# Four integer sums on GpSimd, another order of the first steps, and eight zero products on TensorE in a retention block with a SwiGLU network behind it

## The chip, the cores and the metric

The kernel runs on one core of a Trainium2 chip. A core has five engines that run their own instruction streams and wait for each other on semaphores: TensorE (PE in the profile, with its weight loads as PEld), VectorE (DVE), ScalarE (ACT), GpSimd (POOL) and SyncE (SP), which here only issues DMA transfers. The metric is the device time of one execution in microseconds (us).

## The reference

Two blocks follow each other. The first is a retention recurrence over 4 batches, 8 heads, 768 positions and 64 dimensions:

```python
gamma = 1.0 - 2.0 ** (-5.0 - np.arange(H, dtype=np.float32))
for t in range(S):
    state = gamma[None, :, None, None] * state + np.einsum('bhd,bhe->bhde', k[:, :, t], v[:, :, t])
    y[:, :, t] = scale * np.einsum('bhd,bhde->bhe', q[:, :, t], state)
```

Its output, as x of 3072 rows by 512, goes through a gated network with 1536 hidden columns:

```python
g = x @ w_gate
silu = g * (1.0 / (1.0 + np.exp(-g)))
val = x @ w_val
return (silu * val @ w_out)
```

The weights arrive as 64 bit floats (float64), everything else as 32 bit.

## The kernel before, in words

**Retention in chunks.** The 768 positions of a batch are cut into 6 chunks of 128. In a chunk the recurrence becomes products: scores k times q (step `s`, line L628, then a mask on VectorE, L634), the scores times v (`m`, L713), the old state times the decayed q (`o`, L699), and the update of the state from the decayed k and v (`t`, L684). k is scaled by `k` (GpSimd, L649) or `K` (VectorE), q by `q` or `Q` (L643), the old state by `g` (ACT, L670). Each product is a group of eight instructions in the program, sixteen in the trace. The work is done in 4 segments of 6 chunks (two batches at a time, three chunks of each).

**Numbers in three planes.** To keep 32 bit accuracy, an operand of the large products is split into three rounded planes: for weights `near_a` (ACT, L960), `near_b` (VectorE, L963) and `near_c` (GpSimd, L966), as the steps `n`; for x `far_a` (ACT, L969, inside `m`), `far_b` and `far_c` (VectorE, L399 and L976, the steps `x`). TensorE multiplies plane by plane, so a group of 12 products (3 planes by 4 blocks of 128) needs the third plane for its last four products.

**The first segment** computes gate and value products directly: for the first two hidden blocks of 128 columns in parts, chunk by chunk (`p` for the gate and `v` for the value, L906, twelve products with 256 columns each), then for the other ten in full (`G` and `W`, L888, 384 columns). Later segments use a scheme with seven instead of eight products (L1057), and the down products are L1126.

**Weights from their words.** A 64 bit weight is loaded as two 32 bit words and turned into a 32 bit float on the chip. For a piece, `U` and `V` load words with SP (L511), and the steps `a`, `b`, `S`, `c`, `C` convert them: `a` (ACT, L532) brings the upper word into range, `b` (ACT, L535) puts the sign into PSUM, `S` (VectorE, L545) shifts the bits and joins the sign, `c` (ACT, L538) makes an integer of the upper bits of the lower word, and `C` adds the two as integers. For pieces of the up weights `C` is on VectorE (L553, a custom operation on 16 bit halves), for those of the down weights on GpSimd (L555). The pieces of the first two hidden blocks are converted in two halves of 512 columns each, w_val and w_gate apart (a0:0, a0:1, ...), all others whole.

**What sets the order.** The engines' orders are written out: a text `PLAN` holds 2371 steps, and each step issues its instructions in that place on the engine that it uses. Names with a slash belong to later segments. `l0:2` is the load of operand 2 (0 k transposed, 1 q transposed, 2 v, 3 k by rows) of chunk 0; the first two loads of q are on ACT's queue, all others on SP's. `A0` to `A2` load the tables of masks and decays, `Z` writes converted weights back to DRAM, `T` forms sums of weights (L399), `u` and `y` are the gate's activation and product, `h0` copies a mask for later (L738), `L` loads two small tables. A DMA transfer has one of eight semaphores, used in turn; a transfer waits at its issue for the one eight places earlier to have landed. Ahead of the plan stand a warm-up of eight products of zeros (L1222) and the loading of an activation table.

Of the kernel before, what the change touches and what calls it, by code (L numbers as in the profile page):

```python
# [14 lines left out]
AF = mybir.ActivationFunctionType  # L15
# [10 lines left out]
L = 3  # L26
# [24 lines left out]
    l0:0 l1:0 A0 A1 s0 U0:0 l0:2 l0:3 a0:1 s1 b0:1 A2 h0 S0:1 m0 K0 x0:2 c0:1 l2:0 x0:1 l2:1 l1:3  # L51
    C0:1 t0 l1:2 V0:0 l3:1 n0:0 s2 a0:0 Q2 l3:0 l2:3 n0:1 b0:0 S0:0 m1 k1 x1:1 x1:2 l2:2 c0:0 n0:2
    U1:1 C0:0 t1 o2 l3:3 g2 s3 n0:3 n0:4 l4:1 p0:0 m2 a1:1 x2:1 k2 q3 b1:1 l4:0 a1:0 x2:2 S1:1 l5:1
    l3:2 n0:5 c1:1 k3 t2 C1:1 o3 b1:0 l5:0 l4:2 g3 v0:0 s4 S1:0 t3 l5:2 c1:0 C1:0 U2:0 m3 s5 U12:3
    U3:1 q5 q4 u0:0 a2 o5 o4 T0:0 n1:0 m4 b2 y0:0 x3:1 x3:2 m5 T0:1 n1:1 n1:3 T0:2 S2 n1:2 p0:1 v0:1
    n1:4 T1:0 x4:1 u0:1 y0:1 a12 n1:5 x5:1 U4:0 T1:1 a3 p1:0 x4:2 u1:0 p1:1 x5:2 Z0 u1:1 T1:2 c12
    v1:0 U5:1 y1:0 v1:1 p0:2 Z1 l5:3 v0:2 c2 C2 b12 y1:1 p1:2 n2:0 a4 U6:0 u0:2 b3 n2:1 u1:2 v1:2
    S12 n2:3 L y0:2 S3 c3 n2:2 U13:2 G2:0 n2:4 T2:0 G2:1 C3 y1:2 T2:1 n3:0 b4 n2:5 n3:1 i2:0 i2:1
    T2:2 W2:0 j2:0 n3:2 W2:1 G3:1 n3:3 S4 C12 a5 Z2 j2:1 Z12 n3:4 c4 C4 U7:1 n3:5 T3:0 T3:1 c13 T3:2
    G3:0 n4:0 n4:1 b5 S5 n4:2 W3:0 n4:3 W3:1 i3:0 i3:1 n4:4 a13 a6 G4:1 c5 Z3 b13 G4:0 T4:0 U8:0 C5  # L60
    T4:1 j3:1 n4:5 b6 U14:3 W4:1 n5:0 T4:2 n5:1 i4:1 n5:2 n5:3 j3:0 S6 i4:0 a7 c6 n5:4 W4:0 T5:0 C6
    G5:1 Z4 T5:1 n6:0 U9:1 j4:0 n5:5 S13 G5:0 a8 b7 n6:3 T5:2 j4:1 n6:1 c14 C13 W5:1 S7 i5:1 Z5 n6:4
    i5:0 n6:2 j5:1 c7 W5:0 G6:1 n6:5 l4:3 a9 U10:0 C7 n7:0 G6:0 j5:0 i6:1 T6:0 k4 b8 g4 Z13 n7:1
    n7:3 U15:2 S8 n7:2 W6:1 i6:0 c8 n7:4 T7:0 a14 W6:0 C8 T7:1 T6:1 b14 G7:1 U11:1 n8:0 n8:1 n7:5
    i7:1 T6:2 G7:0 j6:0 b9 S14 W7:0 h2 c15 j6:1 Z6 S9 C14 n8:3 c9 n8:2 i7:0 n8:4 W7:1 G8:1 T7:2 C9
    G8:0 j7:0 n8:5 a10 b10 n9:0 j7:1 n9:3 Z14 a15 W8:0 P2 W8:1 Z7 n9:4 k5 b15 i8:0 S10 T8:0 n9:1
    i8:1 U16:3 n9:5 c10 S15 P0 T8:1 n9:2 C10 a11 C15 G9:0 t4 G9:1 P1 T9:0 i9:0 T8:2 Z15 j8:1 g5 j8:0
    t5 W9:1 W9:0 b11 n10:0 U17:2 T9:1 c16 Z8 n10:3 1/was0.0 a16 i9:1 n10:1 n10:4 n10:2 b16 G10:1 S11
    n10:5 c11 S16 i10:1 G10:0 0/h0.0 j9:0 C16 Z16 C11 n11:0 W10:0 n11:3 a17 j9:1 i10:0 0/h0.1 b17
    T9:2 n11:4 T11:0 Z9 n11:1 T11:1 W10:1 n11:2 G11:1 T11:2 0/W0 n11:5 c17 Z11 0/h1.0 G11:0 j10:0  # L70
    0/d0.0 h1 0/h0.2 1/sc0 j10:1 i11:0 0/h1.1 0/W1 S17 0/d1.0 i11:1 0/d0.1 1/l3 C17 T10:0 1/dec0.0
    W11:0 0/d1.1 0/d0.2 W11:1 0/h2.0 j11:0 0/D0.2 j11:1 1/k0.0 1/l4 1/dec0.1 1/q0.0 0/D0.1 1/q0.1
    0/D0.4 1/k0.1 1/l5 0/D0.0 0/h2.1 0/d1.2 0/h1.2 0/h4.0 0/W2 0/Z0 1/A0 1/y0.06 1/new0.0 0/h4.1
    1/y0.01 0/D0.5 0/D0.3 0/d2.0 1/B0 0/D1.1 0/h3.0 1/y0.03 0/D1.5 1/y0.04 0/Z1 1/y0.02 1/y0.07
    1/y0.05 T10:1 1/was0.1 1/y0.15 1/y0.00 1/y0.14 0/d2.1 0/D1.4 1/y0.12 0/d2.2 0/D1.2 1/y0.13 0/W3
    Z17 0/D1.3 0/Z2 0/d3.0 0/D1.0 0/h2.2 0/h3.1 1/C0 0/W4 T10:2 0/h3.2 0/d3.1 0/h4.2 Z10 1/y0.16
    1/l7 1/y0.17 1/new0.1 1/sum0.0 0/D2.3 0/D2.1 1/y0.10 0/h5.0 1/begin 1/sum0.1 0/d3.2 0/h5.1
    1/y0.11 0/D2.5 1/sc1 0/D2.0 0/d4.0 1/was1.0 0/D2.4 0/d4.1 0/D3.4 1/l6 1/dec1.1 0/h5.2 1/dec1.0
    0/D2.2 1/x0.2.0 0/D3.1 1/q1.1 0/d4.2 0/W5 0/D3.5 1/x0.1.0 0/h6.0 1/k1.0 0/Z3 1/sum0.3 1/k1.1
    1/sum0.2 1/x0.2.1 0/D4.5 0/D3.2 0/D3.3 0/D3.0 1/q1.0 0/Z4 0/h6.1 0/D4.0 0/D4.4 1/x0.1.2 1/x0.1.1  # L80
    1/A1 1/x0.0.0 0/d5.0 1/x0.2.2 1/y1.00 0/h6.2 1/y1.06 1/x0.0.2 1/new1.0 0/D4.2 0/d5.1 0/d5.2
    0/D4.3 0/D4.1 1/y1.07 1/y1.01 0/W6 0/h7.0 1/B1 1/x0.0.1 1/y1.04 1/y1.12 0/h7.1 1/l9 0/d6.0
    0/D5.4 0/h8.0 0/d6.1 1/y1.02 0/D5.3 0/D5.2 0/W7 0/h8.1 1/y1.05 0/d6.2 1/l8 1/l11 0/Z5 1/y1.03
    1/was1.1 0/D5.5 1/C1 0/d7.0 1/y1.16 0/d7.1 0/D6.5 0/D5.0 1/y1.17 1/y1.15 1/new1.1 0/h7.2 1/y1.14
    1/y1.11 0/D5.1 1/y1.13 1/x1.2.0 0/D6.3 0/d7.2 0/D6.4 0/Z6 1/y1.10 0/D7.3 0/h9.0 1/sc2 0/h8.2
    1/x1.2.2 0/D6.2 1/q2.1 1/k2.1 0/D7.5 0/W8 1/sum1.0 0/D6.1 1/sum1.2 1/k2.0 0/D6.0 0/D7.1 1/x1.1.0
    0/h10.0 0/h9.1 0/d8.0 0/D7.2 1/dec2.0 1/l10 1/sum1.1 1/dec2.1 0/W9 1/x1.1.1 0/D7.0 0/d8.1
    1/x1.2.1 0/Z7 1/sum1.3 1/was2.0 1/q2.0 1/x1.0.0 1/x1.1.2 0/d9.0 0/D7.4 0/d8.2 0/h11.0 1/A2
    1/new2.0 0/D8.0 1/x1.0.1 0/h10.1 0/D8.3 0/D8.2 0/d9.1 1/L0 0/D8.1 1/y2.00 0/D8.4 1/B2 0/W10
    0/d9.2 1/y2.07 1/y2.05 0/d10.0 0/D8.5 0/h9.2 1/y2.02 0/h11.1 0/D9.3 1/y2.03 0/h10.2 1/y2.01  # L90
    0/D9.5 0/Z8 1/y2.04 1/y2.06 1/w0.0.0 0/D9.4 0/d10.1 0/h11.2 1/C2 1/y2.16 1/y2.14 0/W11 1/y2.12
    0/D9.1 1/y2.10 0/D9.2 1/L1 0/d10.2 0/D10.3 0/Z9 0/d11.0 1/y2.17 1/x1.0.2 1/y2.15 1/y2.13 0/D9.0
    1/L2 0/D10.4 0/D10.1 1/sum2.2 0/D10.2 0/D10.0 1/y2.11 0/d11.1 1/sum2.0 0/d11.2 1/x2.1.0 1/sum2.1
    1/x2.1.2 1/sum2.3 0/D11.1 0/Z11 1/w0.1.0 0/D11.0 1/x2.0.0 0/D11.3 0/D10.5 0/D11.4 1/w0.0.1
    0/D11.2 1/w0.0.2 1/w1.0.0 1/x2.1.1 1/x2.0.1 0/Z10 1/w1.0.1 0/e0 1/x2.0.2 1/w1.0.2 0/D11.5 1/p0.0
    1/u0.0 1/p0.1 1/p0.2 1/p1.0 1/x2.2.0 1/u0.1 1/w0.2.0 0/e2 1/x2.2.1 1/w0.1.1 1/p1.1 1/x2.2.2 0/e1
    1/w0.1.2 0/e3 1/w1.2.0 1/w1.1.0 1/w0.2.1 1/u1.0 1/w2.1.0 1/u0.3 1/p1.2 1/w1.1.1 1/p0.3 1/u0.4
    1/p0.4 1/w0.2.2 1/u0.5 1/p0.5 1/u0.6 1/w1.2.1 1/w2.0.0 1/w1.1.2 1/u1.3 1/p0.6 1/u0.8 1/p1.3
    1/w2.0.1 1/p1.4 1/u1.4 1/w2.0.2 1/u1.1 1/L3 1/u0.9 1/p1.5 1/p2.0 1/w2.2.0 1/w1.2.2 1/u1.5
    1/w3.2.0 1/u0.2 1/w2.1.1 1/w3.2.1 1/u1.2 1/w3.1.0 1/u1.6 1/u2.0 1/w3.0.0 1/w3.0.1 1/p1.6  # L100
    1/w2.1.2 1/p2.1 1/p2.3 1/w3.1.1 1/L4 1/p2.2 1/u1.8 1/u2.4 1/u2.1 1/u2.3 1/p2.5 1/w3.0.2 1/w4.2.0
    1/u1.9 1/u2.6 1/w2.2.1 1/p2.4 1/w3.2.2 1/L5 1/p3.1 1/w2.2.2 1/u2.5 1/u1.7 1/w4.1.0 1/w4.0.0
    1/u0.7 1/p3.0 1/u3.0 1/w3.1.2 1/w4.0.1 1/w4.1.1 1/p2.6 1/p3.2 1/u3.3 1/p3.3 1/p3.4 1/u3.4 1/u2.2
    1/u2.8 1/p3.5 1/u3.1 1/u3.5 1/L6 1/w5.1.0 1/p3.6 1/w4.0.2 1/u2.9 1/w4.1.2 1/u3.6 1/w5.0.0
    1/w4.2.1 1/p4.1 1/w5.0.1 1/p4.0 0/e5 2/begin 1/w5.2.0 1/w5.0.2 1/u3.8 1/p4.3 1/u4.0 1/w5.1.1
    1/u4.4 1/u3.9 1/w5.2.1 1/p4.2 1/u4.3 1/L7 1/u3.2 1/w5.1.2 1/p4.5 1/p5.0 1/u4.1 1/p4.4 1/u4.5
    1/w6.1.0 1/p5.1 1/u5.0 1/w4.2.2 1/w6.0.0 1/w6.1.1 1/p5.2 1/u5.1 1/u4.6 0/e4 1/w6.1.2 1/u2.7
    1/w6.0.1 1/w6.2.0 1/w5.2.2 1/u5.3 1/p4.6 1/p5.3 1/p5.4 1/u5.4 1/u4.8 1/p5.5 1/u5.5 1/L8 1/w7.2.0
    1/p5.6 1/u4.9 1/w6.0.2 1/u4.2 1/w7.1.0 1/w8.2.0 1/p6.1 1/u5.6 1/w7.0.0 1/u4.7 1/w7.2.1 1/p6.0
    1/u3.7 1/w7.1.1 1/w7.0.1 1/u6.0 1/w8.2.1 1/u5.2 1/u6.1 1/L10 1/p6.3 1/w7.0.2 1/u6.4 1/u5.8  # L110
# [1198 lines left out]
```

## Time and profile before

| what | value |
|---|---|
| runs | 642.94 us median of 3 (642.76 to 645.4) |
| the profiled execution's own time | 642.91 us |
| its span in the profile | 641.1 us |
| TensorE busy | 631.2 us (98%) |
| VectorE, ScalarE, GpSimd busy | 485.6, 392.2, 265.4 us |
| moved by DMA | 140.13 MB, mean 219 GB/s |
| start of p0:1 on TensorE | 32.02 us |

All times in the profile count from the start of the span. The span is 1.8 us shorter than the execution's time, for what lies around it. A row of a timeline merges neighbouring instructions of one kind and gives their start, their length, the engine, the line, the operation, the tiles and shapes, how many there are, and in brackets the idle time of the engine before them with what ended it.

### The profile page before, as it was taken

How to read it: one execution, taken by the hardware profiler on the slowest of the kernel's cores; microseconds unless marked ns; L12 is line 12 of the kernel's file. 1: busy time of each engine (PE TensorE's matmuls, PEld its weight loads, DVE VectorE, ACT ScalarE, POOL GpSimd, SP SyncE). 2: the span in 40 equal slices, each digit the busy share in tenths (PEclk: the TensorE clock that was granted, in tenths of full speed). 3: DMA queues.
4: the chain of work that ended last, by engine and by line, in shares of the span. 5: the costliest groups of instructions: out<-in, count | busy, mean ns of one | idle time of the engine just before them, and what ended most of it. 6: DMA issues, size and time to landing. Idle time of an engine off the chain costs nothing.

```text
span 641.1 us, 14110 instructions
## 1 busy us (share of the span) xinstructions
PE 631.2 (98%) x5579; PEld 579.5 (90%) x5579; DVE 485.6 (76%) x713; ACT 392.2 (61%) x860; POOL 265.4 (41%) x174
## 2 busy tenths in 40 slices
PE   6999999999999999999999999999999999999997
PEld 6899999988779999997778999998777999999886
DVE  5887888999898887665787869675789866768351
ACT  3687697777865565566766555564785555654221
POOL 0535455544427865630002665550101666663000
PEclk9999999999999999999999999999999999999999
DMA  9998978689887445258775540467777444304554
GB/s 322 375 359 295 356 264 301 267 306 319 269 278 290 168 148 173 73 180 260 246 240 214 199 160 10 183 196 243 228 240 263 157 164 172 116 0 153 193 184 178
DMA packets 50626, 140.13 MB, mean 219 GB/s; under 512 B 4992, under 2 KB 17792, under 8 KB 50560
## 3 DMA queue, kind: packets, MB, share of 16 engines
q1 hardware_dynamic: 49984, 138.44, 62.8%
q8 instruction: 44, 0.72, 0.5%
q10 hardware_dynamic: 576, 0.79, 0.3%
q14 instruction: 22, 0.18, 0.1%
HBM read 109.32 MB, written 29.88 MB: 217 GB/s over the span
## 4 chain that ended last, share of the span: by engine, by line
PE 94%; DMA 4%; ACT 0%; DVE 0%; SPq 0%; issue 0%; ACTq 0%
PE bank L1057 41%; PE bank L1126 31%; PE bank L888 13%; PE bank L758 6%; PE bank L906 2%; DMA rawp<-in_w_gate_dram 1%; DMA oitem<-wdnt 1%; DMA hT<-in_k_n_dram 1%; DMA hT<-in_q_t_dram 1%; PE bank L713 0%; PE bank L684 0%; PE bank L699 0%; PE bank L628 0%; SPq L464 0%; DVE bank L545 0%
## 5 line engine op out<-in xcount | busy, mean ns | idle before, releaser
L1126 PE MATMUL bank<-oitem,gitem 128*128 128x512 f32 x867 | 208.4, 394 | 0.5 <-DMA oitem<-wdnt 0.3
L1126 PEld LDWEIGHTS bank<-oitem,gitem 128*128 128x128 f32 x867 | 159.6, 188 | 35.2 <-DMA oitem<-wdnt 0.7
L966 POOL TENSOR_TENSOR gitem<-gitem 128x768 fp32r<-128x768 f32 x72 | 142.0, 1982 | 115.3 <-DVE gitem L963 96.3
L1057 PE MATMUL bank<-xa,gitem 128*128 128x384 f32 x864 | 160.5, 334 | 0.0
L1057 PEld LDWEIGHTS bank<-xa,gitem 128*128 128x128 f32 x864 | 150.8, 188 | 0.2
L966 POOL TENSOR_TENSOR oitem<-oitem 128x256 fp32r<-128x256 f32 (+1 forms) x60 | 65.9, 1106 | 53.7 <-DVE oitem L963 53.3
L1057 PE MATMUL bank<-xb,gitem 128*128 128x384 f32 x432 | 84.5, 334 | 0.0
L888 PE MATMUL bank<-xa,oitem 128*128 128x384 f32 x480 | 84.2, 335 | 0.0
L963 DVE SCALAR_TENSOR_TENSOR gitem<-gitem,loads 128x768 fp32r<-128x768 f32 x72 | 76.0, 1070 | 9.9 <-ACT gitem L960 8.4
L888 PEld LDWEIGHTS bank<-xa,oitem 128*128 128x128 f32 x480 | 83.0, 188 | 0.2
L1057 PEld LDWEIGHTS bank<-xb,gitem 128*128 128x128 f32 x432 | 75.9, 188 | 0.4
L960 ACT ACTIVATE gitem<-loads 128x768 fp32r<-128x768 f32 x72 | 59.6, 843 | 26.0 <-PE bank L1057 16.8
L963 DVE SCALAR_TENSOR_TENSOR gitem<-gitem,hT 128x768 fp32r<-128x768 f32 x48 | 46.2, 965 | 26.1 <-ACT gitem L960 26.1
L960 ACT ACTIVATE gitem<-hT 128x768 fp32r<-128x768 f32 x48 | 40.2, 842 | 32.8 <-PE bank L1126 30.7
L991 ACT COPY chunk_x<-bank 64x128 f32<-64x128 f32 x144 | 36.6, 260 | 31.8 <-PE bank L758 21.2
L399 DVE SCALAR_TENSOR_TENSOR gitem<-gitem 128x768 fp32r<-128x768 f32 x48 | 48.8, 1025 | 0.8
L785 POOL TENSOR_TENSOR loads<-loads,tab 128x512 f32<-128x512 f32 x9 | 13.3, 1479 | 81.8 <-PE bank L758 58.4
L1057 PE MATMUL bank<-xb,oitem 128*128 128x384 f32 x216 | 43.4, 335 | 0.0
L1057 PEld LDWEIGHTS bank<-xb,oitem 128*128 128x128 f32 x216 | 37.9, 188 | 0.3
L1074 DVE TENSOR_TENSOR hT<-bank,tmp 128x384 f32<-128x384 f32 x36 | 20.0, 555 | 20.4 <-PE bank L1057 20.2
L1072 ACT COPY tmp<-bank 128x384 f32<-128x384 f32 x36 | 17.2, 478 | 28.3 <-PE bank L1057 19.3
L963 DVE SCALAR_TENSOR_TENSOR oitem<-oitem,loads 128x256 fp32r<-128x256 f32 (+1 forms) x42 | 33.8, 808 | 0.9 <-ACT oitem L960 0.8
(114 smaller groups left out, 785.7 us busy)
## 6 DMA issues: line engine op xcount, KB each, us to landing
loads<-wup SPq DMA_DIRECT2D x36, 896.0 KB, 4.6
oitem<-wdnt SPq DMA_DIRECT2D x33, 768.0 KB, 4.4
wdnt<-oitem SPq DMA_DIRECT2D x12, 768.0 KB, 6.1
wup<-first SPq DMA_DIRECT2D x9, 896.0 KB, 6.0
rawp<-in_w_gate_dram SPq DMA_DIRECT2D x12, 512.0 KB, 7.2
rawp<-in_w_val_dram SPq DMA_DIRECT2D x12, 512.0 KB, 6.3
rawp<-in_w_out_dram SPq DMA_DIRECT2D x12, 512.0 KB, 7.3
out_dram<-chunk_x SPq DMA_DIRECT2D x21, 256.0 KB, 2.2
```

The lines of the kernel that those rows point to most:

```text
L399: stt(o, x, 1.0, y, op0=mul, op1=op)
L758: nc.tensor.matmul(o, a, b, start=start, stop=True, skip_group_check=True)
L785: (pool if i else both)(t, t, qdec, op=mul)
L888: nc.tensor.matmul(o, w[:, a, ts(b, P)], X0[:, a, i, NC - 1 - b], start=a == b == 0, stop=a == 2 and b == NC - 1, skip_group_check=True)
L960: act(o[0], x, AF.Copy, scale=CUT / FAR)
L963: stt(o[1], f32(o[0]), -FAR, x, op0=mul, op1=add)
L966: op(o[2], f32(o[0]), f32(o[1]), op=add)
L991: copy(cx[half[i], ds(2 * h, 2), c, half[z]], y.rearrange("p (b t) -> p b t", b=2))
L1057: nc.tensor.matmul(o, w[:, a, k], x[:, a, KH - 1 - k], start=start and a == k == 0, stop=a == 2 and k == KH - 1, skip_group_check=True)
L1072: steps = (lambda: copy(p1, x), lambda: tt(c11, z, p1, op=add), lambda: act(gate, c11, AF.Silu, scale=ONE), lambda: copy(u2, x), lambda: c ...
L1074: lambda: copy(p5, wb), lambda: tt(h1, x, p5, op=add),
L1126: nc.tensor.matmul(banks[tok][:, cols], hs[f][:, a, ds(i * TH + u * P, P)], wo[f][:, a, cols], start=f == a == 0, stop=f == NF - 1 and a = ...
```

## The change

Only the first steps of the plan differ: the 160 steps of before up to the first `G2:0` and what stands around it become 168, with the eight steps `w` added; the other 2211 steps are the same. In the new order the tables are loaded ahead of k, k and q of chunk 2 come ahead of k by rows of chunk 0, the w_val words of the first hidden block come later, the loads of chunk 4 stand ahead of the words of the second hidden block, and TensorE does s2 ahead of t0, s4 ahead of the first p and v, and m5 ahead of m4.

The halves are now converted as the down pieces are: `S` leaves its result in SBUF, `c` writes into the raw words' place, and `C` is GpSimd's integer sum. There are four such halves. A step `w` is one product of zeros (128x128) into a bank that is not yet in use: w0 to w4 before s0, w20 to w22 after m0, with the eight of the warm-up still ahead. A step `E` is defined and not used by the plan.

```diff
 PLAN = """
-    l0:0 l1:0 A0 A1 s0 U0:0 l0:2 l0:3 a0:1 s1 b0:1 A2 h0 S0:1 m0 K0 x0:2 c0:1 l2:0 x0:1 l2:1 l1:3
-    C0:1 t0 l1:2 V0:0 l3:1 n0:0 s2 a0:0 Q2 l3:0 l2:3 n0:1 b0:0 S0:0 m1 k1 x1:1 x1:2 l2:2 c0:0 n0:2
-    U1:1 C0:0 t1 o2 l3:3 g2 s3 n0:3 n0:4 l4:1 p0:0 m2 a1:1 x2:1 k2 q3 b1:1 l4:0 a1:0 x2:2 S1:1 l5:1
-    l3:2 n0:5 c1:1 k3 t2 C1:1 o3 b1:0 l5:0 l4:2 g3 v0:0 s4 S1:0 t3 l5:2 c1:0 C1:0 U2:0 m3 s5 U12:3
-    U3:1 q5 q4 u0:0 a2 o5 o4 T0:0 n1:0 m4 b2 y0:0 x3:1 x3:2 m5 T0:1 n1:1 n1:3 T0:2 S2 n1:2 p0:1 v0:1
+    A0 A1 l0:0 l1:0 A2 w0 w1 w2 w3 w4 s0 l0:2 U0:0 l2:1 l2:0 l0:3 l1:3 l1:2 s1 a0:1 l3:1 K0 b0:1
+    c0:1 S0:1 l3:0 m0 w20 w21 w22 k1 l2:3 C0:1 V0:0 s2 l2:2 l4:1 l4:0 t0 Q2 g2 m1 n0:0 U1:1 x0:1 s3
+    t1 l3:3 l3:2 n0:1 l5:1 o2 x1:2 q3 a0:0 b0:0 c0:0 o3 S0:0 k2 l5:0 n0:2 C0:0 g3 n0:3 m2 x1:1 x0:2
+    n0:4 a1:1 t2 b1:1 s4 p0:0 a1:0 l4:2 n0:5 k3 v0:0 S1:1 b1:0 l5:2 x2:2 S1:0 c1:1 m3 t3 q4 c1:0
+    U2:0 s5 q5 C1:1 n1:0 C1:0 x3:1 L x2:1 o4 u0:0 a2 o5 n1:3 m5 n1:1 x3:2 U12:3 m4 x5:2 p0:1 b2 n1:4
...
                 for o, cols in signs_of(piece, half):
                     act(o.bitcast(I32), d[:, cols], AF.Prelu, scale=2.0 ** 94, alpha=2.0 ** 127)
             else:
-                to = d if piece[0] == "up" else lo
+                to = d if piece[0] == "up" and half is None else lo
                 act(to.bitcast(I32), lo, AF.Copy, scale=2.0 ** -29)
...
-                stt(o if piece[0] == "up" else u[:, cols], u[:, cols], 3, o,
+                stt(o if piece[0] == "up" and half is None else u[:, cols], u[:, cols], 3, o,
                     op0=ALU.logical_shift_left, op1=ALU.bitwise_or)
...
-            if piece[0] == "up":
+            if piece[0] == "up" and half is None:
                 tt(d, signs_of(piece, half)[0][0].bitcast(I32), d, op=add)
             else:
                 pool(d, d, lo, op=add)
...
+        "E": lambda n: scale_k_act(cs[n]),
...
-        "L": lambda n: local_k(), "h": lambda n: local_part(n),
+        "L": lambda n: local_k(), "h": lambda n: local_part(n), "w": lambda n: warm_up(1),
...
+    def scale_k_act(c):
+        kd = chunks[c][3].rearrange("p (h d) -> p h d", h=H)
+        for h in range(H):
+            act(kd[:, h], kd[:, h], AF.Copy, scale=kdec[:, ds(h, 1)])
```

## The prediction

> **What bounds the kernel now.** I read the page's busy line first, then the table of windows, then TensorE's timeline up to 33 us, then the queue of SP over the same stretch, and last the rows of the halves of the first weights. The busy line and the windows (columns: stretch, its length, then busy time and instructions of PE, PEld, DVE, ACT, POOL, then the granted clock, the DMA share and GB/s):
>
> ```profile
> PE 631.2 (98%) x5579; PEld 579.5 (90%) x5579; DVE 485.6 (76%) x713; ACT 392.2 (61%) x860; POOL 265.4 (41%) x174
> ...
> 0.00:5.00 5.00, 3.83 (x18) 3.54 (x18) 0.19 (x1) 1.49 (x2) 0.20 (x4) 1.00 0.64 193
> 5.00:30.00 25.00, 20.22 (x312) 18.07 (x312) 19.54 (x33) 14.32 (x30) 9.39 (x8) 1.00 1.07 377
> 30.00:50.00 20.00, 20.00 (x177) 19.71 (x174) 18.26 (x31) 16.32 (x24) 6.22 (x4) 1.00 1.04 362
> 50.00:130.00 80.00, 80.00 (x542) 79.05 (x542) 67.49 (x95) 62.27 (x97) 42.95 (x27) 1.00 0.81 292
> ```
>
> TensorE never rests between 30 and 130 us. Its idle time lies before that: 1.17 us of the first 5 and 4.78 us of the next 25, 5.95 us together. In those 25 us the DMA engines are full (share 1.07). So the change, which alters only the first steps, can gain at most a part of 5.95 us (0.9% of the span); everything later keeps its order and moves with the time at which TensorE's unbroken run begins. That time is 32.02 us, the start of p0:1, in TensorE's timeline (start, length, what, and in brackets the idle time before it):
>
> ```profile
> 9.75 1.09 PE L713 MATMUL bank<-tmp,hT 128*64 128x128 f32 x16 [2.45 <-DMA hT<-in_v_n_dram]
> 11.81 0.69 PE L684 MATMUL bank<-hT 128*64 128x64 f32 x16 [0.96 <-DVE hT L649]
> ...
> 17.70 1.70 PE L906 MATMUL bank<-xa,oitem 128*128 128x256 f32 x12
> 19.33 1.09 PE L713 MATMUL bank<-tmp,hT 128*64 128x128 f32 x16
> 20.26 0.63 PE L684 MATMUL bank<-hT 128*64 128x64 f32 x16
> 20.82 1.09 PE L699 MATMUL bank<-loads,states 64*64 64x128 f32 x16
> 21.84 1.69 PE L906 MATMUL bank<-xa,oitem 128*128 128x256 f32 x12
> 24.18 1.16 PE L628 MATMUL bank<-hT 64*128 64x128 f32 x16 [0.65 <-DMA hT<-in_k_t_dram]
> 25.65 0.69 PE L684 MATMUL bank<-hT 128*64 128x64 f32 x16 [0.30 <-DVE first L553]
> ```
>
> The last real wait is for k_t of chunk 4. SP's queue tells when each load lands: eight transfers are open at a time, so an issue that had to wait starts when the one eight places earlier has landed.
>
> ```profile
> 8.95 0.38 SPq L511 DMA_DIRECT2D rawp<-in_w_val_dram  x1
> ...
> 15.20 0.34 SPq L464 DMA_DIRECT2D hT<-in_q_t_dram  x1
> 15.87 0.33 SPq L464 DMA_DIRECT2D hT<-in_k_t_dram  x1
> 16.56 0.33 SPq L464 DMA_DIRECT2D first<-in_q_t_dram  x1
> 17.23 0.75 SPq L464 DMA_DIRECT2D hT<-in_v_n_dram  x1
> 19.03 0.33 SPq L464 DMA_DIRECT2D first<-in_k_t_dram  x1
> ```
>
> Landings come every 0.67 us for 256 KB and 1.5 us for a 512 KB weight block (13.70 to 15.20), one after another. One step is 1.80 instead of 0.67 (17.23 to 19.03): the DMA view of 16.3 to 19.1 us shows one packet of the instruction queue there, and everything behind it is 1.13 us late.
>
> **The change part by part.** *Order of the loads.* Counting places in the queue (ACT's two q loads with them), the first 14 are the same set before and after, and so are the first 27 and 29; the bytes of the start don't change. By place, after: k_t of chunk 0 is fifth (in before A0, landed at 6.74), k_t of chunk 1 sixth (7.45), n of chunk 0 twelfth (12.3, in before ninth at 10.3). The first w_val block moves from place 15 to 18, behind q3, k3 and n2: the same set as before's first 18, landed at 17.23, plus the 1.13 if the packet comes at the same point, 18.35. v2 stays 19th, 19.03. k_t of chunk 4 moves from 24 to 21, ahead of the two word blocks of the second hidden block (U1): 19.03 + 2 x 0.67 = 20.4 instead of 24.05. The last five (k5, v4, v5 among them) land as before, until 27.4. So the wait of 0.65 at 24.18 goes, and what is late next is the first w_val block, 3.15 us later than the 15.20 of before.
>
> *TensorE up to the unbroken run*, with the durations of its timeline. s0 starts at 6.8 rather than 4.95, s1 ends at 9.0; the masks on DVE (four in 2.52 us) let m0 start at 9.2 instead of 9.75. s2 waits for k_t 2 at 11.65; t0 waits for n0 at 12.3 and its product on DVE (0.69), 13.1 instead of 11.81. m1 13.75, s3 15.1 (k_t 3 at 15.05), then t1, o2, o3 at 0.6 + 1.02 + 1.02 end at 18.9; m2 at 19.05 behind v2, t2 20.0, s4 20.55 to 21.65 without a wait, p0:0 21.65, and v0:0 at 23.3 (1.63 from start to start, as 17.70 to 19.33). Its first eight products need 1.0, until 24.3.
>
> *The second w_val half and the GpSimd sum* lie on the path. After the landing at 18.35 these rows of ACT's and GpSimd's timelines, and the one of the source view of L555 (duration of the shortest, median and longest in ns), give the steps:
>
> ```profile
> 15.21 0.67 ACT L532 ACTIVATE first<-rawp 128x512 f32<-128x512 f32 x1 [0.99 <-DMA rawp<-in_w_val_dram]
> 15.91 0.60 ACT L535 ACTIVATE bank<-first 128x512 int32<-128x512 f32 x1
> ...
> 20.90 1.27 POOL L966 TENSOR_TENSOR oitem<-oitem 128x512 fp32r<-128x512 f32 x1 [1.15 <-DVE oitem L963]
> ...
> L555 POOL TENSOR_TENSOR first<-first,rawp x6: 2440/2518/2892, 51.7 to 128.4; 128x1024 int32<-128x1024 int32 x6
> ```
>
> 0.67 + 0.60 on ACT, 0.69 for the bits on DVE (the 128x512 rows of L545; ACT's third step, 0.69, runs beside it), then the sum on GpSimd. That operation is in the trace at twice the width, 2.44 to 2.89 us; half of the median is 1.25. It replaces 0.68 on DVE (L553) in each of four halves, 2.7 us less for DVE, which hides nothing that TensorE waits for except on this chain. Then 0.62 (L960), 0.69 (L963), 1.27 (L966). The sum is 5.79 and seven hand-overs of about 0.04, 6.05 us: the third plane stands at 24.4. So v0:0 ends at 24.9 whether it waits 0.1 or not: the loads' path and the weights' path arrive together.
>
> *From there* m3, t3, s5, o4, o5, m4, m5 follow, seven groups that took 25.65 to 32.02 in before (t3, m3, s5, and so on), 6.37 us. Their inputs (n3 at 24.05 and 1.04 on GpSimd, k5 at 26.1, v4 and v5 by 27.4) are there in time. 24.9 + 6.37 = 31.3, and 0.1 more for the order of p0 and v0 before m3; I take 31.4. Gain: 32.02 - 31.4 = 0.6 us.
>
> *The zero products.* Eight in before took 3.78 us; five more, at the 0.47 each of a clock not yet released, end at 7.2 at the latest, 0.4 behind k_t 0 at 6.8. That shift ends in the wait for k_t 2 (11.65), as s1 and m0 would end at 10.6. The three behind m0 lie in that same wait. The granted clock is 1.00 in every window of before, with waits up to 2.45 us, so I count nothing for them: between 0 and 0.4, nearer to 0.
>
> *The four sums' price.* Lower end 1.04 (GpSimd's 128x512 product of L649), upper end 2.25: half of 2.52 stretched as the 768 wide row of L966 is at its worst, 3.29 against 1.85. I take 1.25, from the same operation. By the Trainium skill (SBUF — State Buffer, Who interferes with whom) a VectorE instruction with two SBUF inputs shuts out a GpSimd one that reads SBUF for its whole length. By that rule each of the two GpSimd steps on the chain could lose one 0.6 us slot of DVE, and the time would be 643.5, close to the third rival's. The trace agrees in part: L966 at 128x512 is 1.27 at best and 1.80 at worst, but GpSimd's eight rows before 30 us all stand at 1.04 to 1.30, with DVE busy beside most of them.
>
> *Everything else* (the copy of L738 moved behind p0:1, two small loads moved forward, the second hidden block's sums behind the q scalings) is hidden: the second hidden block's third plane is needed at 34.3 + 1.0, and its chain ends near 32.
>
> **Sum.** The profiled execution took 642.91 (span 641.1 and 1.8 around it), the median of the runs is 642.94. 642.91 - 0.6 = 642.3 us.
>
> **Rivals.** (1) As worked out: 642.3, chance 0.54. (2) The packet of the instruction queue, which follows TensorE's instructions, comes earlier or later and delays neither w_val nor v2: these come 1.13 us sooner, and the path up to m5 with them, up to 1.1 more: 641.2. For it speaks that eight more products shift the point; against it, that TensorE has done about as many products at 16 us as in before. 0.15. (3) Slower: the GpSimd sum and L966 behind it keep v0:0 waiting. It decides from 0.6 us over my price; at the ends (2.25 and 1.80) the plane is 1.0 + 0.5 late, and the time is 642.3 + 1.5 = 643.8. For it: the 1.71 and 1.80 rows of L966 after 35 us; against it: the eight rows of GpSimd before 30 us, none over 1.30. 0.13. (4) The head start isn't passed on, as DVE (18.26 of 20 us from 30 to 50) and full DMAs set the pace of the weights: 642.9. Against it: the plane for G2 is ready at 44.7 (L966 at 43.45) and TensorE takes it at 46.5. 0.09. (5) Something else, by over 0.5%: 0.04 faster, 0.05 slower.
>
> **How the numbers follow.** 0.5% is 3.2 us, about what a measurement of this kernel tells from no change. The gain can't reach it unless more than half of all idle time went, and the slower rival stays within it: so rivals 1 to 4 make up the 0.91 of no change, and what lies beyond is left to causes that I don't see (one of the runs shown stands at 645.4). The range goes from the second rival less 0.3 (TensorE's groups at their shortest), 640.9, to the third, 643.8.
>
> **What would show it.** TensorE's p0:1 starts at 31.4 (30.3 in rival 2, over 32.0 in rival 3); s4 starts behind t2 without a wait; the sums of L555 at 128x512 take 1.25; the step of 1.8 between landings falls on w_val or v2; no wait over 0.3 from 32 to 180 us. The prediction is wrong if TensorE waits in v0:0 for GpSimd's third plane (near_c) by more than 0.6, if a new wait opens behind 32 us, or if the clock drops in a wait.

## The result, and the profile after

| | median us | runs | ratio to the kernel before, 95% interval |
|---|---|---|---|
| kernel before | 644.01 (642.35 to 647.33) | 22 | |
| changed kernel | 646.04 (643.54 to 649.63) | 22 | 1.0033 [1.0022, 1.0043] |

The changed kernel is 2 us slower: less than 0.5%, but on the other side of the kernel before than forecast and outside the range of 640.9 to 643.8. The kernel before came out 1.1 above the 642.91 from which the prediction counted, so of the 3.7 us by which 646.04 lies above the forecast of 642.3, the change itself accounts for 2.6: the loss of 2.0 and the missing gain of 0.6. The profiled execution of the changed kernel took 648.01 us (span 646.0), among the longest of the 22, so a second profile of the same kernel (644.67, span 642.7) is read beside it. Its lines stand one to six lower in the file: L906 is L912 now, L888 is L894, L1126 is L1132, L966 is L972.

The busy line of the page after:

```profile
PE 636.0 (98%) x5595; PEld 582.2 (90%) x5595; DVE 485.8 (75%) x709; ACT 392.4 (61%) x860; POOL 270.7 (42%) x178
```

and the windows after (columns as before):

```profile
5.00:30.00 25.00, 23.58 (x340) 21.02 (x340) 18.11 (x30) 14.04 (x30) 14.70 (x12) 1.00 1.07 375
30.00:50.00 20.00, 20.00 (x169) 19.83 (x166) 16.27 (x28) 14.98 (x22) 5.75 (x5) 1.00 0.87 305
50.00:130.00 80.00, 78.36 (x531) 76.96 (x530) 68.46 (x96) 63.45 (x98) 41.66 (x27) 1.00 0.86 304
```

TensorE now idles 1.42 us instead of 4.78 between 5 and 30, but 1.64 between 50 and 130, where it never rested before. And from 30 to 50 the DMA engines are busy 0.87 of the time instead of 1.04. TensorE's timeline shows the head as forecast, and then the new wait:

```profile
11.91 1.16 PE L629 MATMUL bank<-hT 64*128 64x128 f32 x16 [0.75 <-DMA hT<-in_k_t_dram]
...
20.39 1.16 PE L629 MATMUL bank<-hT 64*128 64x128 f32 x16
21.48 3.44 PE L912 MATMUL bank<-xa,oitem 128*128 128x256 f32 x24
...
31.23 1.94 PE L912 MATMUL bank<-xa,oitem 128*128 128x256 f32 x14
...
68.34 2.89 PE L894 MATMUL bank<-xa,oitem 128*128 128x384 f32 x15 [1.64 <-DVE hT L442]
```

s4 (20.39) follows t2 without a wait, and p0:0 and v0:0 are one row of 24 products, so v0:0 doesn't wait for its third plane. p0:1 starts at 31.23, 0.79 ahead of before. At 68.34 that is lost, and more. Matching each of TensorE's instructions in the two traces gives the changed kernel's lag on before: -0.79 until 66 us, +1.12 behind it, +1.94 behind 140, +3.2 behind 200, +4.9 at the end. In the second profile it is -0.57, -0.18, +1.41, +1.2 and +1.6. The losses at 66 and 140 are in both.

The chain of waits over 30 to 70 us (start, length, what) says where the first comes from:

```profile
53.12 2.43 POOL first L555
...
56.90 8.11 DMA rawp<-in_w_gate_dram
...
65.11 1.13 ACT first L538
...
66.26 1.22 DVE first L553
67.49 0.33 DVE first L399
67.82 0.48 DVE hT L442
```

The transfer is U7, the words of hidden block 7; L538 is c5. In the plan of both kernels c5 stands behind U7, which goes into the place of block 5's words, so c5 waits for that load (and, in both kernels, takes block 7's lower words in the place of block 5's). In before U7 landed at 60.09 and 61.42 and c5 ran without waiting; now U7 lands at 63.65 and 65.00. ScalarE's row of c5, in before:

```profile
62.32 1.15 ACT L538 ACTIVATE first<-rawp 128x1024 int32<-128x1024 uint32 x1
```

and after:

```profile
65.11 1.12 ACT L538 ACTIVATE first<-rawp 128x1024 int32<-128x1024 uint32 x1 [2.86 <-DMA rawp<-in_w_gate_dram]
```

The product that waits starts 3.23 behind c5's start, and 3.24 or 3.25 behind it in the four other profiles that show a wait of 0.25 or more at this place. TensorE of before reached this product at 67.49 (66.70 and the 0.79 that it is ahead now), so c5 had 1.9 in hand there. It starts 2.79 later now, and with the 0.79 that makes the wait of 1.64.

SP's queue after shows how the words of the early blocks came to be late:

```profile
25.50 1.06 SPq L511 DMA_DIRECT2D rawp<-in_w_out_dram  x2
31.54 0.38 SPq L511 DMA_DIRECT2D rawp<-in_w_val_dram  x1
32.02 0.47 SPq L511 DMA_DIRECT2D rawp<-in_w_gate_dram  x1
32.53 0.50 SPq L511 DMA_DIRECT2D rawp<-in_w_val_dram  x1
...
42.24 0.38 SPq L511 DMA_DIRECT2D rawp<-in_w_val_dram  x1
```

and the same stretch in before:

```profile
24.06 1.42 SPq L511 DMA_DIRECT2D rawp<-in_w_out_dram  x2
28.04 0.38 SPq L511 DMA_DIRECT2D rawp<-in_w_val_dram  x1
...
31.75 0.37 SPq L511 DMA_DIRECT2D rawp<-in_w_val_dram  x1
...
37.61 0.37 SPq L511 DMA_DIRECT2D rawp<-in_w_val_dram  x1
```

Between 26.56 and 31.54 SP now stands before U4, which waits for a2; U3, which before was issued at 28.04, ahead of U4, follows at 32.53. The last open transfer lands at 32.82 and the next at 35.40, so the DMA engines run dry. U3 lands at 40.99 instead of 36.35, a3 starts at 41.07 instead of 36.43, and U5, which waits for a3, is issued at 42.24 instead of 37.61.

### The profile page after: what moved, and what is told of

Read it like the earlier page. It is cut to its first block, busy times and chain, and to the rows that moved or that the text cites. A ratio compares the mean times of both kernels' runs of the same rounds, so it can differ in the third digit from the quotient of the medians.

```text
span 646.0 us, 14153 instructions
## 1 busy us (share of the span) xinstructions
PE 636.0 (98%) x5595; PEld 582.2 (90%) x5595; DVE 485.8 (75%) x709; ACT 392.4 (61%) x860; POOL 270.7 (42%) x178
## 4 chain that ended last, share of the span: by engine, by line
PE 87%; DMA 6%; DVE 3%; POOL 1%; ACT 1%; issue 1%; SPq 0%; ACTq 0%; POOLq 0%; DVEq 0%
PE bank L1063 40%; PE bank L1132 29%; PE bank L894 10%; PE bank L764 5%; DMA oitem<-wdnt 2%; PE bank L912 2%; DMA rawp<-in_w_gate_dram 1%; DMA wdnt<-oitem 1%; DMA hT<-in_k_n_dram 1%; DMA hT<-in_q_t_dram 1%; POOL first L555 1%; DVE xa L399 1%; DVE oitem L969 0%; DMA oitem<-wdn 0%; PE bank L719 0%
## 5 line engine op out<-in xcount | busy, mean ns | idle before, releaser
L1132 PE MATMUL bank<-oitem,gitem 128*128 128x512 f32 x867 | 209.0, 395 | 1.8 <-DMA oitem<-wdnt 1.4
L1132 PEld LDWEIGHTS bank<-oitem,gitem 128*128 128x128 f32 x867 | 159.4, 188 | 37.1 <-DMA oitem<-wdnt 2.2
L972 POOL TENSOR_TENSOR gitem<-gitem 128x768 fp32r<-128x768 f32 x72 | 141.0, 1967 | 116.7 <-DVE gitem L969 96.5
L972 POOL TENSOR_TENSOR oitem<-oitem 128x256 fp32r<-128x256 f32 (+1 forms) x60 | 65.6, 1100 | 52.7 <-DVE oitem L969 48.7
L894 PE MATMUL bank<-xa,oitem 128*128 128x384 f32 x480 | 84.6, 335 | 1.6 <-DVE hT L442 1.6
L894 PEld LDWEIGHTS bank<-xa,oitem 128*128 128x128 f32 x480 | 83.0, 188 | 2.3 <-DVE hT L442 2.0
L966 ACT ACTIVATE gitem<-loads 128x768 fp32r<-128x768 f32 x72 | 59.6, 842 | 24.7 <-PE bank L1063 16.7
L966 ACT ACTIVATE gitem<-hT 128x768 fp32r<-128x768 f32 x48 | 40.2, 841 | 33.3 <-PE bank L1132 31.2
```

Of the source, the lines that this page charges most:

```text
L894: nc.tensor.matmul(o, w[:, a, ts(b, P)], X0[:, a, i, NC - 1 - b], start=a == b == 0, stop=a == 2 and b == NC - 1, skip_group_check=True)
L966: act(o[0], x, AF.Copy, scale=CUT / FAR)
L972: op(o[2], f32(o[0]), f32(o[1]), op=add)
L1132: nc.tensor.matmul(banks[tok][:, cols], hs[f][:, a, ds(i * TH + u * P, P)], wo[f][:, a, cols], start=f == a == 0, stop=f == NF - 1 and a = ...
```

## The experiments

Theory A: the new order brings the words of the early blocks late, and that, not the head, decides. Rivals: B, the wait was that execution's own; C, the GpSimd sums and their hold on the raw words cost; and from the second group on D, the zero products cost.

**Does the wait come back?** The changed kernel once more, without an edit.

> The changed kernel once more, to see which of its waits come back. Theory A (the new order delivers the words of hidden blocks 3 and 4 late, in every execution): p0:1 starts at 31.2 again, and TensorE waits again at 66 to 69 us, for 1.2 to 2.0 us, in G5/W5's row behind the conversion of hidden block 5; the time is 1.0 to 3.0 us above the kernel before. Theory B (the wait was this one execution's own, slow transfers by chance): p0:1 at 31.2, no wait over 0.6 between 60 and 75 us, and the head start of 0.8 is still there at 100 us. The waits of 0.4 to 0.9 us behind 180 us are expected to differ from those of the first profile by both.

Measured: 645.42, ratio 1.0038 [1.0023, 1.0053]. p0:1 starts at 31.45. No wait of 0.25 or more stands between 30 and 140 us in this profile, but TensorE still lost 0.4 at 66, c5 waited 0.89 for U7 (landed at 63.70) and U5 was issued at 42.06: the lateness is the order's own, the size of the wait varies. A larger loss stands at 140, which no theory had:

```profile
139.70 0.73 PE L1132 MATMUL bank<-oitem,gitem 128*128 128x512 f32 x2
141.66 3.92 PE L1132 MATMUL bank<-oitem,gitem 128*128 128x512 f32 x16 [1.23 <-issue]
```

"Issue" means that the engine waited for nothing that the profile shows. A packet of the instruction queue (16 KB) starts at 139.41 and takes 0.96 us, ending right before the gap.

**The order.** U3 alone put ahead of U4:

```diff
-    v0:1 u0:1 n1:2 y0:0 U4:0 p1:0 S2 u1:0 T0:0 x4:2 T0:1 n1:5 h0 y0:1 U3:1 p1:1 T0:2 v1:0 a12 x4:1
+    v0:1 u0:1 n1:2 y0:0 U3:1 U4:0 p1:0 S2 u1:0 T0:0 x4:2 T0:1 n1:5 h0 y0:1 p1:1 T0:2 v1:0 a12 x4:1
```

> The changed kernel with one load moved: the words of block 3 (U3:1) are issued ahead of those of block 4 (U4:0), as in the order before. Theory A: U3's first issue moves from 32.5 to about 30.2 (when GpSimd's sum lets go of its place), its landings from 39.5 and 41.0 to about 34.5 and 36, block 4's from 35.4 and 36.9 to about 38; a3 starts near 39.8 instead of 41.07, because ScalarE's c2 ahead of it now waits for block 4; the wait near 66.7 falls from 1.64 to 0.3 to 0.5 and the time by 1.2 (0.8 to 1.6) against the changed kernel. Theory B: the time stays that of the changed kernel within 0.4. Theory C (it is GpSimd's sums and their hold on the words' places that cost): no more than 0.4 is won.

Measured: 646.29, 1.0054 [1.0039, 1.0068]: no gain. U3 was issued at 30.44 and landed at 34.82 and 36.28 as expected, but ScalarE's c2 stood ahead of a3 and waited 1.24 for U4 (39.24), a3 started at 40.67, U5 was issued at 41.84, and TensorE waited 1.00 at 67. Moving the load alone is not enough; the step that takes its words, a3, has to move on ScalarE too. So, on top of that edit:

```diff
-    v1:1 y1:0 c2 x5:1 u1:1 p0:2 l5:3 v0:2 a3 T1:0
+    v1:1 y1:0 a3 c2 x5:1 u1:1 p0:2 l5:3 v0:2 T1:0
```

> The changed kernel with two steps in the places of the order before: block 3's words are issued ahead of block 4's, and ScalarE's a3 stands ahead of c2, which waits for block 4's words. Moving the words alone didn't help, as a3 stayed at 40.7 behind c2 and block 5's words, which wait for a3, at 41.8. Theory A (the late a3 hands its delay on by U5, c3, U6, C12, U7 to c5 and so to TensorE at 67): a3 starts at 38 to 38.5, U5 is issued at 39 to 39.7 instead of 42, U7 lands at 61.5 to 63 instead of 63.7 to 65.0, no wait over 0.4 between 50 and 75 us, and the head start of 0.6 to 0.8 stands until 139 us. The zero products still make TensorE stand at 140 (0.5 to 1.5). Time 0.5 to 1.5 below the changed kernel. Rival (the transfer of block 7 behind the writes to DRAM is slow by itself, wherever a3 stands): U7 lands past 63.5 and the wait of 0.4 to 1.6 near 67 stays.

Measured: 644.30, 1.0009 [0.9995, 1.0023], 1.5 to 1.9 below the changed kernel by the ratios (1.0009 against 1.0033 and 1.0038), 1.1 to 1.7 by the medians. a3 started at 38.53 and U5 was issued at 39.69. The profiled execution is the slowest of this kernel's eleven (645.90), and in it U7 landed at 63.21 and 64.53, later than expected; TensorE waited 0.33 at 67 and lost 1.3 at 140. So the time bears A out, this profile only half, and it doesn't exclude the rival named there, that U7 is slow wherever a3 stands: TensorE, whose p0:1 started at 32.08 here, came later to the product too. Next, the wait of c5 for U7 taken away from its other side:

```diff
-... Z12 n3:4 c4 C4 U7:1 n3:5 ... a13 a6 G4:1 c5 Z3 b13
+... Z12 n3:4 c4 C4 n3:5 ... a13 a6 G4:1 c5 Z3 U7:1 b13
```

> The changed kernel with the words of block 7 (U7:1) issued behind c5 and Z3 instead of ahead of them. In both kernels c5 stands in the plan behind the load that overwrites the words which it reads, so it waits for that load to land and takes block 7's lower words; here it takes block 5's own and waits for no load. Theory A: c5 runs at 62.3 behind a6, the wait of TensorE near 67 is under 0.3, U7 is issued at 63.4 and lands by 67.5, ahead of a7 (70.3); time 0.4 to 1.6 below the changed kernel, the stand at 140 stays. Rival (the delay sits elsewhere: VectorE or a13 and a6 are late too): a wait of 0.5 or more remains at 66 to 69 us. If U7 at 67.5 is too late for what follows, a new wait opens between 75 and 95 us.

Measured: 650.74, 1.0113 [1.0097, 1.0128]. The wait at 67 is gone, as expected of A. What was named as a risk happened: U7 is issued at 65.09, U8 behind it, and c6, which stands behind U8 as c5 did behind U7, waits on ScalarE's timeline

```profile
70.46 1.16 ACT L532 ACTIVATE loads<-rawp 128x1024 f32<-128x1024 f32 x1 [1.25 <-DMA rawp<-in_w_gate_dram]
74.16 1.13 ACT L538 ACTIVATE first<-rawp 128x1024 int32<-128x1024 uint32 x1 [2.54 <-DMA rawp<-in_w_gate_dram]
```

and TensorE waits 2.82 at 76.58. Both edits together:

> The changed kernel with both of these edits. Theory A: as the better of the two within 0.4, as each takes the same wait away; the head start of 0.6 to 0.8 stands until 139 us, then 0.5 to 1.5 are lost at 140. Time 0.2 below to 0.8 above the kernel before.

Measured: 649.45, 1.0098 [1.0084, 1.0113], with 3.52 at 75.22: the same new wait; and without the zero products

> Both of these edits, and without the eight zero products. Theories A and D together: no stand of 0.4 or more at 140, no wait over 0.4 from 32 to 180 us; the head start is 0.0 to 0.3 as without the products alone (p0:1 at 31.8 to 32.1). Time 642.5 to 643.5, 0.3 below to 0.2 above the kernel before. If the waits of 0.4 to 0.7 at 53 us come back (block 5's words landing at 50.3), the supply of words is late for another reason than a3.

647.25, 1.0062 [1.0049, 1.0075], 3.44 at 75.02, and no stand at 140. At both places looked at the kernel hangs on when words land: before had 2.8 in hand between the landing of U7 and TensorE's need (0.9 and 1.9), and at c6, by the same reckoning, 1.3 (U8 landed at 69.25, c6 started at 69.35; the product follows c6 by 5.23 in these three profiles, and before reached it at 75.81).

**The sums.** First the four half sums put back on VectorE in the new order, by the conversion of before:

```diff
-                to = d if piece[0] == "up" and half is None else lo
+                to = d if piece[0] == "up" else lo
...
-                stt(o if piece[0] == "up" and half is None else u[:, cols], u[:, cols], 3, o,
+                stt(o if piece[0] == "up" else u[:, cols], u[:, cols], 3, o,
...
-            if piece[0] == "up" and half is None:
+            if piece[0] == "up":
```

The halves then share one PSUM bank for their shifted bits, and in this order the second half overwrites the first's before it is summed, so this kernel's weights of the second hidden block are not the reference's.

> The changed kernel with the four half sums back on VectorE (the conversion of the halves as before), order and zero products as changed. Theory A: block 3's words still stand behind block 4's, which wait for a2 at 31.5, so U3 is issued at 32.5 as in the changed kernel; the wait at 66.7 stays at 1.2 to 2.0; the head is as early or up to 0.6 earlier (a half's sum 0.69 instead of 1.30), p0:1 at 30.6 to 31.3; the time is that of the changed kernel less 0 to 0.6. Theory C (the sums cost): U3 early, the wait near 66.7 under 0.5, the time 1.5 or more below the changed kernel.

Measured: 647.74, 1.0077 [1.0062, 1.0092]. Both theories missed: TensorE's o4 waits 2.68 us at 28.74 for a sum on VectorE (L553), and everything is 3.2 late from there; nothing is told of the words. By the kernel's text o4 writes the very bank that holds the shifted bits. What the run does show is that the new order doesn't go together with the sums of before. The other way round, these three edits turned about in the kernel before, which puts the sums on GpSimd in the old order and changes nothing else:

> The kernel before with one part of the change alone: the four half sums on GpSimd, in the old order and without the zero products. In the old order the second half's sum ends right ahead of TensorE's v0:0 (idle 0.30 at 25.65), so each theory puts 0.6 (1.30 instead of 0.69) there: p0:1 at 32.6 instead of 32.02. Theory A: nothing more, as U3 is issued only about 0.6 to 1.2 later (28.6 to 29.3): the time is 0.6 (0.2 to 1.0) above the kernel before, and no wait over 0.5 opens between 60 and 75 us. Theory C: U3's words come 2 or more later and a wait of 1 us or more opens at 60 to 75 us; the time is 1.6 or more above.

Measured: 647.70, 1.0070 [1.0055, 1.0084], 4.5 over before and neither theory's figure. No wait opens at 60 to 75; the loss lies in the head. GpSimd's timeline:

```profile
24.55 1.29 POOL L555 TENSOR_TENSOR first<-first,rawp 128x512 int32<-128x512 int32 x1
28.28 1.28 POOL L555 TENSOR_TENSOR first<-first,rawp 128x512 int32<-128x512 int32 x1 [2.44 <-issue]
29.53 1.26 POOL L643 TENSOR_TENSOR loads<-first,tab 128x512 f32<-128x512 f32 x1
30.76 1.72 POOL L643 TENSOR_TENSOR loads<-hT,tab 128x512 f32<-128x512 f32 x1
```

The sum takes 1.28, as priced, but it waits in its queue, and the q scalings of chunks 5 and 4 behind it start at 29.53 and 30.76 instead of 24.79 and 26.02. TensorE waits for them, 2.04 and 0.59, and the granted clock falls to 0.62 to 0.69 from 30 to 40 us. In the new order these scalings stand ahead of the last sums (25.08 and 26.32, the sums at 27.57), and none of this happens. So C falls as the cause of the changed kernel's loss: its order keeps the sums out of the scalings' way. What stays of C is that the sums hold U3's place: with U3 put first it is issued at 30.27 to 31.18 in seven profiles, when the last sum ends, against 28.04 in before. In the kernel with both causes out, below, this costs nothing that shows.

**The zero products.** The changed kernel without them:

```diff
-    A0 A1 l0:0 l1:0 A2 w0 w1 w2 w3 w4 s0 ...  m0 w20 w21 w22 k1
+    A0 A1 l0:0 l1:0 A2 s0 ...  m0 k1
```

> The changed kernel without its eight zero products. Theory D (the zero products are not free: they move TensorE's instruction stream, so that a packet of the instruction queue is fetched at 62.2 to 62.5 us, in the middle of the transfer of block 7's words, instead of at 64.7, and so that TensorE stands at 140 us, in the third product of an L1132 group, for a packet of its own instructions): the packet comes at 63.5 to 64.5, the wait near 66.7 falls to 0.6 or less, TensorE doesn't stand at 140 (0.4 and 1.2 in the two profiles of the changed kernel), and the time is 1.5 to 2.5 below the changed kernel. Theory A (only the order makes words late): both waits stay within 0.4 of the two profiles of the changed kernel, and so does the time. Third (the products held the clock): the granted clock falls between 5 and 15 us, and p0:1 starts 0.5 or more later than 31.2.

Measured: 645.15, 1.0021 [1.0005, 1.0038]. The packet came at 66.38 instead of 62.5, TensorE didn't stand at 140 (lag 1.45 on both sides of it), and the profiled execution, at 647.59 one of its slowest, lost 1.2 between 53 and 67 and 1.74 at 199.4 waiting for GpSimd (L972). So D holds at 140 and falls at 67, where the waits don't need the packet. The time fell by 0.8 to 1.1 by the ratios, where D expected 1.5 to 2.5, and the interval overlaps that of the changed kernel, so this run alone shows no gain. The clock stayed at 1.00 from 5 to 20 us; p0:1, at 31.86, was late through k_t of chunk 2, which landed at 12.43. The products alone, in the kernel before:

```diff
-    l0:0 l1:0 A0 A1 s0 U0:0 ... S0:1 m0 K0
+    l0:0 l1:0 A0 A1 w0 w1 w2 w3 w4 s0 U0:0 ... S0:1 m0 w20 w21 w22 K0
```

> The kernel before with the eight zero products alone, five ahead of s0 and three behind m0, the old order and the sums on VectorE. All theories: p0:1 at 32.0 (within 0.2), as the products lie in the waits of 2.45 and 0.96. Theory D: the instruction packet comes at 63.3 or so instead of 64.7, still behind block 7's words (landed at 61.4), so no wait at 67; but TensorE stands 0.4 to 1.5 at 140 us, and the time is 0.4 to 1.5 above the kernel before. Theory A: within 0.3 of the kernel before, no wait at 140.

Measured: 644.73, 1.0025 [1.0013, 1.0038], 1.6 over before. p0:1 at 31.94, no wait at 67, and on TensorE's timeline

```profile
139.68 0.73 PE L1126 MATMUL bank<-oitem,gitem 128*128 128x512 f32 x2
141.51 3.94 PE L1126 MATMUL bank<-oitem,gitem 128*128 128x512 f32 x16 [1.10 <-issue]
```

where before has one row:

```profile
139.80 4.38 PE L1126 MATMUL bank<-oitem,gitem 128*128 128x512 f32 x18
```

The lag jumps from -0.11 to +1.28 there and stays. With sixteen in the changed kernel:

```diff
-    A0 A1 l0:0 l1:0 A2 w0 w1 w2 w3 w4 s0 ... m0 w20 w21 w22 k1
+    A0 A1 l0:0 l1:0 A2 w0 w1 w2 w3 w4 w5 w6 w7 w8 w9 s0 ... m0 w20 w21 w22 w23 w24 w25 k1
```

> The changed kernel with sixteen zero products instead of eight, ten ahead of s0 and six behind m0. Five more ahead of s0 take up to 2.3 and push s1 to 11.3, still ahead of k_t of chunk 2 at 11.8; m0 and three more (0.5) may come 0.5 late: p0:1 at 31.2 to 31.9. Theory D: the packets come another eight products (1.4 us in this stretch) earlier, at 61 instead of 62.4; the wait near 66.7 stays over 0.5, and the one at 140 changes its size or its place by more than 0.4. Theory A: nothing changes behind 60 us by more than the head's shift.

Measured: 647.03, 1.0057 [1.0039, 1.0074]; the stand is 1.81 at 140.23, in the L764 products ahead of the group, and the lag grows by 3.7 over these few microseconds. More products, a longer stand, earlier in TensorE's program. Then the changed kernel without the products and with U3 ahead of U4:

> The changed kernel without the zero products and with block 3's words ahead of block 4's. Theory D: as without the zero products alone, within 0.5, since at 57 us block 7's words are issued no earlier with U3 first (57.0 against 56.9); the time is 0.3 to 1.0 below the kernel before if nothing else waits. Theory A: 0.8 or more below the one that only leaves the products out.

Measured: 645.24, 1.0024 [1.0010, 1.0038], as without the products alone, and no stand at 140.

All nine profiles with added products lose at 140 (0.4 to 3.7), none of the others does. The sixteen profiles show ten idle times of TensorE of 0.2 or more behind 32 us that "issue" ends, seven near 140 with added products and three near 184 without; each of the ten ends 1.3 to 1.6 us behind the end of a 16 KB packet of the instruction queue. That TensorE waits there for its own instructions is the reading that fits; the profile names no releaser. Packets start at 138.6 in before and at 139.24 in the kernel before with products, where the products ought to make them due earlier; why the packet doesn't come sooner stays open.

**Both causes out.** The edits of U3, a3 and of the products in one kernel:

> The changed kernel with block 3's words ahead of block 4's, a3 ahead of c2, and without the eight zero products: the two causes taken out, each by the edit that undid it alone. If both are the whole cause and add up: no stand at 140 (in the five profiles without the extra products it was 0, in the nine with them 0.4 to 3.7 of shift), at most 0.4 of waits between 50 and 75 us, and the time of the kernel with U3 and a3 moved less 0.8 to 1.4: 643.0 to 643.5, 0.5 below to 0.2 above the kernel before. If the order has a third price (the copy of L738, k_n of chunk 5 ahead of Z0, the sums' load on GpSimd), the time is 644 or more, and its place shows as a wait behind 32 us.

Measured: 643.54, 1.0001 [0.9992, 1.0010], 2.1 to 2.4 below the changed kernel by the ratios (2.5 and 1.9 by the medians): the 1.5 to 1.9 of the order and the 0.8 to 1.1 of the products add up to it within their intervals. U5 is issued at 39.42, U7's second half lands at 63.06, and behind the wait for k_t of chunk 2, which ends at 12.05, TensorE has no wait of 0.2 or more until 300 us. The profiles agree in the order's part: from 47 to 95 us TensorE loses 0.5 to 2.0 in the six with the sums on GpSimd, U7 in its place and a3 late, and 0.0 to 0.7 in the three with U3 and a3 put back. Within the interval, some 0.6 to each side, the two causes are the whole loss; the 0.3 that the head wins is too small to show in it. Last, the one other transfer that the order put ahead of words:

```diff
-... p0:2 l5:3 v0:2 ... v1:2 Z1 c12
+... p0:2 v0:2 ... v1:2 Z1 l5:3 c12
```

> The same with the load of k by rows of chunk 5 (l5:3) behind Z1, as in the order before, instead of ahead of Z0. It takes 0.65 of the DMA engines ahead of Z0 and the words of block 5. If it is a part of the lateness of words, Z0 and U5 land 0.6 sooner, U7 lands below 62.5, and the time is 0.1 to 0.5 below the same kernel without this edit; if not, the two agree within 0.3.

Measured: 643.02, 0.9996 [0.9987, 1.0005]; U5 and U7 landed no earlier (46.76 and 63.81), and the two kernels can't be told apart. No version measured beats the kernel before.

## Why the prediction was wrong

- *The head.* Right: p0:1 at 31.23 and 31.45 for 31.4, the wait for k_t of chunk 4 gone, the long step between landings on v2 (17.33 to 18.78). The first w_val half landed at 17.33, as the forecast without the packet has it. The plane of v0:0 stood at 24.13 for 24.4, which is luck in part: the first w_val half came 1.0 sooner than counted, and the chain behind it took 6.8 for 6.05, as VectorE took up its step at 19.27, 0.56 behind the end of ScalarE's. And the gain is no larger than what the loads vary by: over the twelve profiles that have this head with the sums on GpSimd, p0:1 starts at 31.2 to 32.8, 31.7 on the mean against 32.02, some 0.3 won.
- *The GpSimd sums.* Right: 1.29 and 1.30 for 1.25, and no wait in v0:0. In two later profiles, of the kernels with U3 and a3 moved and with U7 behind c5, the first w_val half landed at 18.75 and 19.46 and v0:0 did wait for the plane, 0.31 each: the third rival's wait, through a late load and not a long sum. By the rule of the Trainium skill (SBUF — State Buffer, Who interferes with whom) a VectorE instruction with two SBUF inputs and a GpSimd one that reads SBUF contend, and the order of issue decides which of them waits. The trace agrees, and here it was VectorE that waited for a sum: beside the sum from 14.20 to 15.50 VectorE's L644 (two SBUF inputs, begun at 14.90) took 1.15 instead of 0.68, and GpSimd's q scaling, begun at 15.45, took 1.74 instead of 1.30. No sum was stretched; most of what VectorE did beside the sums has an input in PSUM.
- *The zero products.* Wrong: the term "0 to 0.4, nearer to 0" counted only where they stand. There they are hidden, but alone they cost 1.6 us (0.8 to 2.4 by the interval), 130 us later. The second rival saw that they shift instruction packets, and looked for the effect in the first 20 us only.
- *"Everything else is hidden".* This is the step that failed most. The prediction took everything behind p0:1 as unchanged, though the steps that the change moves reach up to the first G2, which TensorE takes at 45.73. It followed the second hidden block's planes to 35 us and SP's queue to 27.4, and never the words of blocks 3 to 7, though the change put U4 ahead of U3, and U4 waits for a2. Followed further, SP's queue would have shown that U3 now stands behind that wait, 5 us long from 26.56. With U3 and a3 put back the time falls by 1.5 to 1.9 by the ratios.
- *Rival 4* had the right kind of cause (the weights' pace, not TensorE's start) and was given 0.09 at no loss: it was weighed at one place, G2's plane, with 1.8 us in hand. At c5 the words of block 7 had 0.9 in hand (61.42 against 62.32), and c5 itself 1.9 before TensorE's need. And it allowed the gain to be lost, not more.
- *"No wait over 0.3 from 32 to 180 us"* was the test that the text set, and it failed: 1.64 at 66.70 and 0.42 at 141.77 in the first profile, 1.23 at 140.44 in the second. The clock did not drop (1.00 in every window), as forecast.
- *What a measurement tells.* The prediction took 0.5% (3.2 us) for it, which was too wide: the interval of the 22 runs is 0.7 us to each side, and the loss of 2 us is clear of it.

## What to carry to other kernels

A reordering of the first steps is also a reordering of every queue behind them: follow each moved load to the consumer that sits furthest down its chain, and ask on each engine's queue what now stands ahead of that consumer, since moving the load alone gained nothing here. A kernel whose bound engine rests nowhere can still have its supply only 1 to 3 us ahead of it, as at c6 and c5 here, so look there before you count on a head start being kept. Instructions that are hidden where they stand still lengthen the engine's stream, and that can cost later, so try such filler alone.

## What was not expected of the hardware

- A stand of TensorE of 0.3 to 1.8 us at 140 us, from products added in the first 12 us, as above. Without them three kernels of the new order show a like stand at 184 us (0.29 to 0.85).
- A load that follows writes to DRAM in the queue can land late: U7's first half lands 2.83 us behind the write ahead of it in before and 3.73 after (1.4 to 4.4 over the eleven other profiles in which it stands there), while 512 KB loads behind loads land mostly every 1.2 to 1.5 us. What delays them is not shown.
- In the kernel before, the zero products hold the clock, and it was worth nothing. In the new order without them the wait for k_t of chunk 2 can be followed by a dip, here in the windows of the kernel with both causes out, where that wait was 1.57:

```profile
12.50:15.00 2.50, 2.50 (x34) 2.28 (x33) 2.12 (x4) 0.43 (x1) 1.66 (x2) 0.50 1.05 383
```

All twelve executions of the kernel before with the products have a mean granted clock of 0.999 or 1.000; of the 77 of the kernel before without them that ran beside the experiments, 49 are lower. Their medians are 643.32 with the lower clock and 643.22 without, so these dips cost nothing that shows; where in the execution they lay is not on record.
